# Retention attention and a two-layer MLP on one core: planner lead, buffers, relu engine, tail order and warm-up matmuls changed together

## The chip, the cores and the metric

The kernel runs on one core of one Trainium2 chip. The metric is the device time of one execution in microseconds. Four executions of the kernel before are given; the median is the number to compare with. One of the four was run under the hardware profiler, and all views of the trace come from that one.

Engine names in the profile: PE is TensorE (PEld its weight loads), DVE is VectorE, ACT is ScalarE, POOL is GpSimd, and SP is SyncE, which only issues DMAs here. A name such as SPq means the instruction queue of an engine.

## What is computed

A linear attention with decay per head (a recurrent state), followed by a layer norm without bias, a two-layer MLP with relu, and a residual sum. Shapes: 4 batches, 8 heads, 768 positions, head dimension 64; the model dimension is 512 and the hidden one 2048.

```python
gamma = 1.0 - 2.0 ** (-5.0 - np.arange(H))
for t in range(S):
    state = gamma[None, :, None, None] * state + np.einsum('bhd,bhe->bhde', k[:, :, t], v[:, :, t])
    y[:, :, t] = scale * np.einsum('bhd,bhde->bhe', q[:, :, t], state)
...
x = y.transpose(0, 2, 1, 3).reshape(B, S, H * D)
xn = (x - mean) / np.sqrt(var + 1e-06) * g_ln
out = x + np.maximum(xn @ w_ch1, 0.0) @ w_ch2
```

## The kernel before

**Tiles.** The 768 positions of each batch are six chunks of 128, so there are 24 tiles of 128 positions. Tiles 0 to 3 are the first chunks of the four batches; then come the chunks 1 to 5 of batch 0 (tiles 4 to 8), of batch 1 (9 to 13), batch 2 (14 to 18) and batch 3 (19 to 23). Within a batch the recurrence is done by chunks: scores inside the chunk, and a carried state for what lies before it.

**Attention of one tile.** q, k and v are loaded by GpSimd's DMA queue with a cast from f32 to bf16 (L338), 128 KB each as bf16. For tiles under 10 (`T0`), k and q are transposed on PE (tk, L394; tq, L401) and evacuated by ACT (trk) and DVE (trq, L406). From tile 10 on, k and q share one buffer `qk` and are transposed by a DMA from SP (tr, L416), after which DVE scales q into trq (eq, L423). Then PE makes the scores (pa, L433), DVE multiplies them by the decay mask into asb (am, L440), and PE makes the output (py: the state part on L452, the chunk's own part on L456). For the next chunk's state GpSimd scales v into vg (L509), PE makes k-transposed times vg (pd, L520), and DVE scales it into the state (pb, L534).

**Norm and MLP.** DVE makes the statistics (L490) and the normed xn (L465), ACT keeps a copy of x (L496). xn is transposed on PE (tx, L548) for tiles under 10, by a DMA from SP (ex, L562) after. The first layer (m1, L595) runs in groups of tiles: six groups of one tile, three of two, three of four. Each result is passed through relu into h, by ACT (L608) or DVE (L610). The second layer of each tile is four parts of four matmuls (m2, L632) that sum into one PSUM buffer of the pool `tp`; DVE scales the sum by 1/std, adds x (L640), and SP stores the tile (L647). The last tile's second layer is done in two column halves, and its second half is stored from ACT's queue.

**The order.** The order on each engine is made by a planner when the kernel is built. Each task has an engine (or a choice of two), a cost in ns, a rank, the tasks that it waits for, and the buffer that it takes. The planner repeatedly picks the task that can start first, and among equals the one of lowest rank; the instructions are then written out in that order, and each engine runs its own in that order. Ranks of MLP tasks are 500 plus a unit count, in which one unit stands for one m1 or m2 piece. `rank_of` (L375 to L378) sets the rank of each tile's attention: a number of units (the lead) ahead of the first m1 of its group. Loads are ranked by their order (L356). vg is ranked just ahead of or behind its tile's attention (L512).

**Buffers.** Pools (L166 to L174) give how many buffers of a kind exist: `qk` has 3, `vsb` 5, `vg` 3; in PSUM `tp` and `mm` have 2, `pa`, `py` and `pd` 1. A load waits until the oldest buffer of its pool is free. Besides, each GpSimd load waits for the landing of an earlier one, eight loads before.

**Zero matmuls.** Where the planner sees PE idle before 20 us, `fill` (L99) puts matmuls on zeros there (L656), as many as the gap divided by a time for each: 110 ns for a gap that begins before 6.5 us, 60 ns after. They write a buffer that nobody reads.

Of the kernel before, what the change touches and what calls it, by code (L numbers as in the profile page):

```python
# [14 lines left out]
PE, ACT, DVE, POOL, SP = range(5)  # L15
# [97 lines left out]
def kernel(  # L113
# [19 lines left out]
    DM = H * D  # L133
# [11 lines left out]
    G0 = [sum(GROUPS[:g]) for g in range(NG)]  # L145
    GMAX = max(GROUPS)
    T0 = 10
# [8 lines left out]
    plan = Plan({PE: 330, ACT: 130, DVE: 130, POOL: 130, SP: 0},  # L156
                {PE: 900, ACT: 800, DVE: 900, POOL: 1300, SP: 800}, 2250, 6000)
    ps = bass.MemoryType.PSUM

    def make_pool(name, n, space=None):  # L160
# [6 lines left out]
        name: make_pool(name, n, space)  # L167
        for name, n, space in (
            ("k0", B, None), ("v0", B, None), ("qsb", 6, None), ("ksb", 5, None), ("vsb", 5, None),
            ("qk", 3, None), ("tr", 4, None), ("vg", 3, None), ("trq", 3, None), ("trk", 3, None),  # L170
            ("asb", 2, None),
            ("xn", 4, None), ("xnt", 4, None), ("h1", 2, None), ("osb", 3, None),
            ("tp", 2, ps), ("pa", 1, ps), ("py", 1, ps), ("pd", 1, ps), ("mm", 2, ps),
# [5 lines left out]
    def take(pool, key, shape, dtype):  # L179
        held[pool, key] = pools[pool].tile(shape, dtype, name=pool, tag=pool)  # L180
        return held[pool, key]
# [88 lines left out]
    a = plan.add  # L270
# [32 lines left out]
    def tile_of(kind, t):  # L303
        if kind != "v" and t >= T0:
            return held["qk", t][:, "qk".index(kind)]
        return held[where[kind, t]]
# [55 lines left out]
    unit, u, behind = {}, 0, []  # L362
# [12 lines left out]
    rank_of = {}  # L375
    for t in range(NT):
        g, i = group_of[t]
        rank_of[t] = 10 * t if t < 4 else max(10 * t, 500 + unit["1", g, 0] - (48 if t < T0 else 56) + 8 * i)  # L378


    ex, pbt, vgs, pbs = {}, {}, [], []
# [1 line left out]
    for t in range(NT):  # L383
        b, c = TILES[t]
        r = rank_of[t]
        g, i4 = group_of[t]
# [114 lines left out]
        if c > 0:  # L501
            for cc in ([0, 1] if c == 1 else [c]):
                if cc == C - 1:
                    continue
                j = number[b, cc]

                def e_vg(eng, j=j, cc=cc):
                    e = nc.gpsimd if eng == POOL else nc.vector
                    e.tensor_tensor(  # L509
                        out=take("vg", j, [P, H, D], BF16), in0=tile_of("v", j),  # L510
                        in1=vsc[:, cc, :].unsqueeze(2).to_broadcast([P, H, D]), op=ALU.mult)
                vgt = a(POOL, 1050, r - 2 if cc == 0 else r + 1, e_vg,  # L512
                        [loaded["v", j], vscd] + vgs[-1:], ("vg", j), [where["v", j]])
                vgs.append(vgt)

                def e_pd(eng, j=j, b=b, cc=cc):
                    if cc == 0:
                        take("pd", b, [P, NPAIR, P], FP32)
                    for i in range(NPAIR):
                        nc.tensor.matmul(  # L520
                            held["pd", b][:, i, :], lhsT=tile_of("k", j)[:, 2 * i:2 * i + 2, :],
                            rhs=held["vg", j][:, 2 * i:2 * i + 2, :],
                            start=(cc == 0 and i == 0), stop=(cc == C - 2), skip_group_check=True)
                pdt = a(PE, 230, r - 1 if cc == 0 else r + 2.2, e_pd,
                        [vgt, loaded["k", j]] + ([pbt[j]] if cc else []),
                        ("pd", b) if cc == 0 else None,
                        [("vg", j), where["k", j]] + ([("pd", b)] if cc else []))

                def e_pb(eng, n=number[b, cc + 1], b=b, cc=cc):

                    held["pb", n] = state[len(pbs) % 2]
                    pbs.append(n)
                    for o in (slice(0, D), slice(D, P)):
                        nc.vector.tensor_tensor(  # L534
                            out=held["pb", n][o, :, o], in0=held["pd", b][o, :, o],
                            in1=gch[o, cc, :].unsqueeze(2).to_broadcast([D, NPAIR, D]), op=ALU.mult)
                pbt[number[b, cc + 1]] = a(
                    DVE, 690, r - 1 if cc == 0 else r + 4, e_pb, [pdt, gchd, zerod],
                    ("pb", number[b, cc + 1]), [("pd", b)])
                if cc == 0:  # L540

                    pyt["after"].append(pbt[t])
# [40 lines left out]
    relu, begun = {}, {}  # L583
    for g in range(NG):
        n = GROUPS[g]
        hb, h0 = buf_of[g]
        two = GMAX // n
        for ho in range(0, HO, two):
            key = ("1", g, ho)

            def e_m1(eng, hb=hb, h0=h0, ho=ho, n=n, two=two, key=key):
                p = take("mm", key, [P, two, n * P], FP32)
                for j in range(two):
                    for ko in range(KO):
                        nc.tensor.matmul(p[:, j, :],  # L595
                                         lhsT=w1[:, ko, (ho + j) * P:(ho + j + 1) * P],
                                         rhs=held["xnt", hb][:, h0:h0 + n, ko, :],
                                         start=(ko == 0), stop=(ko == KO - 1))
            m = a(PE, 865, 500 + unit["1", g, ho], e_m1,
                  [ex[t] for t in range(G0[g], G0[g] + n)] + [loaded["w1", ho // 4]],  # L600
                  ("mm", key), [("xnt", hb)])

            def e_re(eng, hb=hb, h0=h0, ho=ho, n=n, two=two, key=key):
                if ho == 0 and h0 == 0:
                    take("h1", hb, [P, HO, GMAX * P], BF16)
                dst, src = held["h1", hb][:, ho:ho + two, h0 * P:(h0 + n) * P], held["mm", key]
                if eng == ACT:
                    nc.scalar.activation(out=dst, in_=src, func=AF.Relu)  # L608
                else:
                    nc.vector.tensor_scalar_max(out=dst, in0=src, scalar1=0.0)  # L610
            first = ho == 0 and h0 == 0
            relu[g, ho] = a({ACT: 600, DVE: 660} if G0[g] < 12 else ACT,
                            600, -10, e_re, [m] + ([] if first else [begun[hb]]),
                            ("h1", hb) if first else None,
                            [("mm", key)] + ([] if first else [("h1", hb)]))
            if first:
                begun[hb] = relu[g, ho]

    for t, cols in [(t, slice(0, DM)) for t in range(NT - 1)] + [
            (NT - 1, slice(i * DM // 2, (i + 1) * DM // 2)) for i in range(2)]:  # L620
        g, i4 = group_of[t]
        hb, h0 = buf_of[g]
        key = ("tp", ("2", t, cols.start))
        w = cols.stop - cols.start
        dep = [relu[g, ho] for ho in range(0, HO, GMAX // GROUPS[g])]
        prev = None
        for part in range(4):
            def e_m2(eng, hb=hb, i=h0 + i4, key=key, part=part, cols=cols, w=w):
                if part == 0:
                    take(*key, [P, w], FP32)  # L630
                for ho in range(4 * part, 4 * part + 4):
                    nc.tensor.matmul(held[key], lhsT=held["h1", hb][:, ho, i * P:(i + 1) * P],  # L632
                                     rhs=w2[:, ho, cols], start=(ho == 0), stop=(ho == HO - 1))
            prev = a(PE, 865 * w // DM, 500 + unit["2", t] + part, e_m2,
                     dep + [loaded["w2", i] for i in range(4) if part == 0] + ([prev] if prev else []),
                     key if part == 0 else None,
                     [("h1", hb)] + ([key] if part else []))

        def e_add(eng, t=t, key=key, cols=cols, w=w):
            nc.vector.scalar_tensor_tensor(  # L640
                out=take("osb", key, [P, w], FP32), in0=held[key], scalar=rstd[:, t:t + 1],
                in1=x_all[:, t, cols], op0=ALU.mult, op1=ALU.add)
        add = a(DVE, 750 * w // DM, -10, e_add, [prev, held["rs", t]], ("osb", key), [key])

        def e_st(eng, t=t, key=key, cols=cols):
            b, c = TILES[t]
            (nc.scalar if eng == ACT else nc.sync).dma_start(out=out_v[b, c, :, cols],  # L647
                                                             in_=held["osb", key])
        a(ACT if cols.start else SP, 350, 100, e_st, [add], uses=[("osb", key)])
# [7 lines left out]
                             start=True, stop=True)  # L657

    with tc.manual_schedule():
        for t in plan.fill(plan.order(), PE, 1100, 20000, lambda at: 110 if at < 6500 else 60, warm):  # L660
            t["emit"](t["eng"])


# [28 lines left out]
```

## Time and profile before

| | us |
|---|---|
| median of four runs | 222.8 |
| the four runs | 228.59, 222.97, 222.34, 222.63 |
| the profiled one among them | 228.59 |
| its span, first to last instruction | 226.8 |
| matmuls on zeros (L656), 121 of them, busy | 11.2 |
| first layer (L595), 768 matmuls, busy | 95.1 |
| second layer (L632), 400 matmuls, busy | 90.4 |
| DVE relu (L610), 9 of them, mean | 0.688 |
| ACT relu (L608), 87 of them, mean | 0.597 |
| DMA transposes of q and k (tr), 14, median to landing | 5.5 |

Times of instructions count from the span's start. The difference between a run's time and its span (here 1.8) lies around the instructions. Busy time of PE is modelled and overlaps from one matmul to the next, so the step from one start to the next is the better measure: 56 ns for 128 columns, 109 for 256, 216 for 512 at full clock. "In turn" below means in an engine's own order. A landing is the time at which the last of a DMA's completions came, which the trace records for each DMA.

### The profile page before, as it was taken

How to read it: one execution, taken by the hardware profiler on the slowest of the kernel's cores; microseconds unless marked ns; L12 is line 12 of the kernel's file. 1: busy time of each engine (PE TensorE's matmuls, PEld its weight loads, DVE VectorE, ACT ScalarE, POOL GpSimd, SP SyncE). 2: the span in 40 equal slices, each digit the busy share in tenths (PEclk: the TensorE clock that was granted, in tenths of full speed). 3: DMA queues.
4: the chain of work that ended last, by engine and by line, in shares of the span. 5: the costliest groups of instructions: out<-in, count | busy, mean ns of one | idle time of the engine just before them, and what ended most of it. 6: DMA issues, size and time to landing. Idle time of an engine off the chain costs nothing.

```text
span 226.8 us, 4691 instructions
## 1 busy us (share of the span) xinstructions
PE 214.6 (95%) x1955; PEld 135.7 (60%) x1955; DVE 117.7 (52%) x229; ACT 86.9 (38%) x170; POOL 89.5 (39%) x105
## 2 busy tenths in 40 slices
PE   6899899999999999989999399999999999999993
PEld 6499899986856566656667135454444444444452
DVE  6435778987669997587895415583111011110121
ACT  5326579874513332223226124356242343333000
POOL 8995699869643784853865000000000000000000
PEclk9679999999999999999999769999999999999999
DMA  8999999999999999999999951201110111101212
GB/s 146 176 179 178 179 158 205 185 154 157 191 83 162 118 141 140 201 196 183 179 124 159 185 102 46 69 19 30 46 45 1 49 46 46 46 12 37 92 46 92
DMA packets 105127, 26.12 MB, mean 115 GB/s; under 512 B 97810, under 2 KB 102162, under 8 KB 105107
## 3 DMA queue, kind: packets, MB, share of 16 engines
q0 software_dynamic: 75984, 13.24, 76.9%
q1 hardware_dynamic: 27938, 12.20, 26.3%
q10 hardware_dynamic: 1184, 0.39, 0.7%
q8 instruction: 15, 0.25, 0.5%
q14 instruction: 6, 0.04, 0.1%
HBM read 27.27 MB, written 6.29 MB: 148 GB/s over the span
## 4 chain that ended last, share of the span: by engine, by line
PE 85%; DMA 9%; DVE 3%; issue 1%; SPq 0%; ACT 0%; DVEq 0%
PE mm L595 35%; PE tp L632 34%; DMA tr<-qk 7%; PE pa L433 3%; PE mm L656 3%; PE py L456 3%; DMA grow<-in_moe_g_ln_dram 2%; PE pd L520 2%; PE py L452 2%; DVE asb L440 2%; PE tp L394 1%; PE tp L401 1%; PE tp L548 1%; PE mm L291 1%; SPq L324 0%
## 5 line engine op out<-in xcount | busy, mean ns | idle before, releaser
L595 PE MATMUL mm<-xnt,w 128*128 128x128 bf16 (+2 forms) x768 | 95.1, 275 | 0.0
L632 PE MATMUL tp<-w,h 128*128 128x512 bf16 (+1 forms) x400 | 90.4, 372 | 0.0
L608 ACT ACTIVATE h<-mm 128x512 bf16<-128x512 f32 x87 | 51.9, 597 | 84.6 <-PE mm L595 84.1
L595 PEld LDWEIGHTS <-w 128*128 128x128 bf16 x768 | 58.9, 98 | 25.1 <-issue 1.7
L632 PEld LDWEIGHTS <-h 128*128 128x128 bf16 x400 | 38.2, 98 | 39.7 <-issue 1.3
L640 DVE SCALAR_TENSOR_TENSOR osb<-tp,rstd,x_all 128x512 f32<-128x512 f32 (+1 forms) x25 | 18.1, 728 | 67.3 <-PE tp L632 67.1
L440 DVE TENSOR_TENSOR asb<-pa,mask 128x1024 bf16<-128x1024 f32 x24 | 29.3, 1220 | 11.6 <-PE pa L433 11.5
L338 POOL DMA_DIRECT2D vsb<-in_v_dram x20 | 18.0, 901 | 12.3 <-PE py L456 9.0
L509 POOL TENSOR_TENSOR vg<-vsb,vsc 128x512 bf16<-128x512 bf16 x16 | 17.0, 1067 | 11.3 <-DMA vsb<-in_v_dram 3.6
L465 DVE SCALAR_TENSOR_TENSOR xn<-py,mv,gb 128x512 bf16<-128x512 f32 x24 | 18.0, 751 | 0.8
L490 DVE BATCH_NORM_STATS2 bns<-py 128x6 f32<-128x512 f32 x20 | 13.9, 695 | 6.6 <-PE py L456 6.5
L496 ACT CAST x_all<-py 128x512 bf16<-128x512 f32 x20 | 11.7, 583 | 14.4 <-DVE xn L465 14.2
L534 DVE TENSOR_TENSOR state<-pd,gch 64x256 bf16<-64x256 f32 x40 | 16.7, 418 | 0.3
L338 POOL DMA_DIRECT2D qk<-in_k_dram x14 | 12.6, 903 | 3.1 <-DMA tr<-qk 2.7
L338 POOL DMA_DIRECT2D qk<-in_q_dram x14 | 12.5, 891 | 1.6 <-DMA w<-in_moe_w_ch_dram 1.6
L656 PE MATMUL mm<-zeros 128*128 128x128 bf16 x121 | 11.2, 264 | 1.0 <-DVE zeros L218 1.0
L456 PE MATMUL py<-vsb,asb 128*128 128x64 bf16 x160 | 8.1, 195 | 3.9 <-DVE asb L440 3.9
L456 PEld LDWEIGHTS <-asb 128*128 128x128 bf16 x192 | 8.2, 101 | 4.0 <-DVE asb L440 4.0
L656 PEld LDWEIGHTS <-zeros 128*128 128x128 bf16 x121 | 9.9, 122 | 1.2 <-DVE zeros L218 1.0
L423 DVE TENSOR_TENSOR trq<-tr,qsc 128x512 bf16<-128x512 bf16 x14 | 6.2, 445 | 7.1 <-DMA tr<-qk 6.9
L610 DVE TENSOR_SCALAR h<-mm 128x512 bf16<-128x512 f32 x9 | 6.2, 688 | 6.5 <-PE mm L595 6.3
L338 POOL DMA_DIRECT2D qsb<-in_q_dram x9 | 8.1, 895 | 1.9 <-PE tp L401 1.6
(68 smaller groups left out, 133.0 us busy)
## 6 DMA issues: line engine op xcount, KB each, us to landing
out_dram<-osb SPq DMA_DIRECT2D x23, 256.0 KB, 2.0
w<-in_moe_w_ch_dram POOLq DMA_DIRECT2D x8, 512.0 KB, 9.5
vsb<-in_v_dram POOLq DMA_DIRECT2D x20, 128.0 KB, 6.4
qk<-in_k_dram POOLq DMA_DIRECT2D x14, 128.0 KB, 5.6
qk<-in_q_dram POOLq DMA_DIRECT2D x14, 128.0 KB, 5.7
qsb<-in_q_dram POOLq DMA_DIRECT2D x9, 128.0 KB, 8.9
ksb<-in_k_dram POOLq DMA_DIRECT2D x6, 128.0 KB, 9.1
k<-in_k_dram POOLq DMA_DIRECT2D x3, 128.0 KB, 7.4
```

Of the source, the lines that this page charges most:

```text
L338: nc.gpsimd.dma_start(out=tile_of(kind, j), in_=src)
L440: nc.vector.tensor_tensor(out=take("asb", t, [P, NPAIR, 2, P], BF16).rearrange("p i a t -> p a i t"), in0=held["pa", t], in1=mask.rearrang ...
L456: nc.tensor.matmul(py[:, h, :], lhsT=held["asb", t][:, h // 2, h % 2, :], rhs=tile_of("v", t)[:, h, :], start=(mi == 0), stop=(mi == n - 1))
L465: nc.vector.scalar_tensor_tensor(out=take("xn", t, [P, DM], BF16), in0=held["py", t].rearrange("p h d -> p (h d)"), scalar=mv[:, t, 0:1], ...
L490: nc.vector.bn_stats(out=bns[:, t, :], in_=held["py", t].rearrange("p h d -> p (h d)"))
L509: e.tensor_tensor(out=take("vg", j, [P, H, D], BF16), in0=tile_of("v", j), in1=vsc[:, cc, :].unsqueeze(2).to_broadcast([P, H, D]), op=ALU. ...
L534: nc.vector.tensor_tensor(out=held["pb", n][o, :, o], in0=held["pd", b][o, :, o], in1=gch[o, cc, :].unsqueeze(2).to_broadcast([D, NPAIR, D ...
L595: nc.tensor.matmul(p[:, j, :], lhsT=w1[:, ko, (ho + j) * P:(ho + j + 1) * P], rhs=held["xnt", hb][:, h0:h0 + n, ko, :], start=(ko == 0), s ...
L608: nc.scalar.activation(out=dst, in_=src, func=AF.Relu)
L632: nc.tensor.matmul(held[key], lhsT=held["h1", hb][:, ho, i * P:(i + 1) * P], rhs=w2[:, ho, cols], start=(ho == 0), stop=(ho == HO - 1))
L640: nc.vector.scalar_tensor_tensor(out=take("osb", key, [P, w], FP32), in0=held[key], scalar=rstd[:, t:t + 1], in1=x_all[:, t, cols], op0=AL ...
L656: nc.tensor.matmul(held["mm", "warm"][:, 0:P], lhsT=zeros, rhs=zeros, start=True, stop=True)
```

## The change

Six edits are made together.

1. The pool `qk` gets four buffers instead of three.
2. The lead of the attention ahead of its group's first m1 is 48 units for all tiles; before it was 48 for tiles under 10 and 56 from tile 10 on.
3. The vg of tile 4 gets a rank ahead of all remaining loads on GpSimd.
4. DVE may take a relu only for groups that begin before tile 6; before, for groups that begin before tile 12.
5. In the ranks of the last tile's second layer, the parts of the second half come after all of the first half's; before, the two halves took turns.
6. The number of zero matmuls is computed with 110 ns for gaps that begin before 11.5 us and 80 after.

```diff
-            ("qk", 3, None), ("tr", 4, None), ("vg", 3, None), ("trq", 3, None), ("trk", 3, None),
+            ("qk", 4, None), ("tr", 4, None), ("vg", 3, None), ("trq", 3, None), ("trk", 3, None),
...
-        rank_of[t] = 10 * t if t < 4 else max(10 * t, 500 + unit["1", g, 0] - (48 if t < T0 else 56) + 8 * i)
+        rank_of[t] = 10 * t if t < 4 else max(10 * t, 500 + unit["1", g, 0] - 48 + 8 * i)
...
-                vgt = a(POOL, 1050, r - 2 if cc == 0 else r + 1, e_vg,
+                vgt = a(POOL, 1050, -500 if j == 4 else r - 2 if cc == 0 else r + 1, e_vg,
                         [loaded["v", j], vscd] + vgs[-1:], ("vg", j), [where["v", j]])
...
-            relu[g, ho] = a({ACT: 600, DVE: 660} if G0[g] < 12 else ACT,
+            relu[g, ho] = a({ACT: 600, DVE: 660} if G0[g] < 6 else ACT,
                             600, -10, e_re, [m] + ([] if first else [begun[hb]]),
...
-            prev = a(PE, 865 * w // DM, 500 + unit["2", t] + part, e_m2,
+            prev = a(PE, 865 * w // DM, 500 + unit["2", t] + part + (4 if cols.start else 0), e_m2,
                      dep + [loaded["w2", i] for i in range(4) if part == 0] + ([prev] if prev else []),
...
-        for t in plan.fill(plan.order(), PE, 1100, 20000, lambda at: 110 if at < 6500 else 60, warm):
+        for t in plan.fill(plan.order(), PE, 1100, 20000, lambda at: 110 if at < 11500 else 80, warm):
             t["emit"](t["eng"])
```

Because the planner reads ranks, buffers and costs, the edits move tasks on every engine, not only those that they name. In the built order the zero matmuls go from 121 to 86. On GpSimd the vg of tile 4 stands between v of tile 6 and k of tile 7, and k of tile 13 is issued between the vg of tiles 9 and 10. On PE the pd of tile 9 follows directly on the pa of tile 8, where before it followed on the py of tile 8. On DVE the trq of later tiles still stands ahead of the asb of earlier ones in many places, for example those of tiles 14 and 15 ahead of the asb of tile 13. On SP the tr of tiles 21 and 22 follow each other.

## What I predict, before the result

> **What bounds the kernel now.** I read four views in this order: the page, the chain of waits in order of time, the timelines of PE and POOL, and the busy time in stretches. First the page:
>
> ```profile
> span 226.8 us, 4691 instructions
> PE 214.6 (95%) x1955; PEld 135.7 (60%) x1955; DVE 117.7 (52%) x229; ACT 86.9 (38%) x170; POOL 89.5 (39%) x105
> PEclk9679999999999999999999769999999999999999
> ```
>
> PE is the bound: 95% of the span, so a gain has to come out of PE's own work or out of its few gaps. The clock row shows half speed at the start and once more at the 23rd and 24th of the 40 slices. The chain says where PE isn't doing useful work (start, duration, what):
>
> ```profile
> 10.69 2.03 PE mm L656 x19
> ...
> 13.89 2.43 PE mm L656 x36
> ...
> 88.45 8.46 DMA tr<-qk
> ...
> 120.74 6.51 DMA tr<-qk
> 127.27 0.42 DVE trq L423
> 127.72 1.24 DVE asb L440
> 129.00 0.61 PE py L456 x8
> 129.61 3.41 PE mm L595 x8
> 133.03 4.00 PE tp L632 x16
> ```
>
> L656 are matmuls on zeros, which only pass time. The two `tr<-qk` pieces are DMA transposes that the chain followed back to; how much PE lost there is in its timeline, in brackets behind the instruction that waited:
>
> ```profile
> 98.66 0.40 PE L433 MATMUL pa<-trq,tr 64*128 64x128 bf16 x8 [0.95 <-DVE asb L440]
> 129.00 0.61 PE L456 MATMUL py<-vsb,asb 128*128 128x64 bf16 x8 [3.87 <-DVE asb L440]
> ```
>
> So stall 1 (tile 16) costs about 1.1 us from issue to issue, stall 2 (tile 20) 4.0. The name DVE asb hides the cause: in VectorE's order the trq of a later tile (L423, 127.27) stands ahead of the asb of tile 20 (L440, 127.72), and it waits for the transpose of tile 21. After stall 2 eight 512-column matmuls take 3.41 instead of the 1.73 of the chain's other pieces, and the next sixteen 4.00 instead of 3.45: another 2.2. The stretches confirm it (after the busy times: clock, DMA share, GB/s):
>
> ```profile
> 95.00:100.00 5.00, 4.05 (x47) 2.42 (x46) 3.04 (x4) 0.00 (x0) 1.79 (x2) 1.00 1.87 204
> 125.00:130.00 5.00, 1.13 (x13) 0.71 (x11) 2.00 (x3) 0.55 (x1) 0.00 (x0) 0.72 1.71 187
> 130.00:135.00 5.00, 5.00 (x16) 1.83 (x14) 1.28 (x3) 1.67 (x3) 0.00 (x0) 0.60 0.53 107
> ```
>
> **The profiled run isn't the typical one.** It took 228.59 (226.8 of span and 1.8 around it), the other three runs 222.34 to 222.97. Taking stall 2 and its slow clock out, 4.0 + 2.2 = 6.2, leaves 222.4: the other runs fit a kernel with stall 1 and without stall 2. I count from 222.4; the median shown, 222.8, lies 0.4 above.
>
> **What the Trainium skill says.** "TensorE: Matmul & The Clock Gate", Part 1: the clock is full or half, decided over free-running windows of 3413 ns. The trace agrees: its clock record has one half-clock stretch of 6.83 us (two windows) from 127.2, and zeros cost 107 ns each before 14.5 us and 56 after. The page asks for a whole idle window; here 2.0 us idle (125.1 to 127.2) were enough, and the trace decides. "Perfetto Trace Analysis", Per-engine timelines: VectorE and ScalarE are strict FIFO; the trq that held up asb agrees. "DMA: Bandwidth & Descriptors", Issuing engines are not separate DMA queues: loads from GpSimd and transposes from SyncE share 16 engines. It agrees: loads landed 0.6 to 0.9 us apart before 57 us, but 1.8 apart from 91.0 to 96.6 (v17 to q17), with transposes in flight.
>
> **Part by part.**
>
> *Fewer zeros.* 121 become 86. Those that go: 9 before the first py, 1 and 17 before tile 2's transposes, then 2, 2, 1 and 3. The first py could go when asb of tile 0 was ready at 11.0 (9.76 + 1.23); nineteen zeros kept it until 12.71, ten end at 11.76: 0.95 gained. Nineteen in place of 36 then run to 14.7 instead of 16.3, the data of tile 2 having landed at 12.3; behind them the k and xnt evacuations on ScalarE (0.58 each) just keep up. Tile 0's first L595 comes at about 16.25 instead of 17.90, the second at 18.6 instead of 20.40. So PE is 1.8 ahead at 20 us. The weights don't hold it: the third quarter of w1 landed at 22.4 and is used from 23.3.
>
> *Where that goes.* GpSimd is paced by landings until 56 us: each load waits for the landing of the eighth before it, and loads land back to back.
>
> ```profile
> 46.16 0.87 POOL L338 DMA_DIRECT2D qk<-in_q_dram  x1 [1.63 <-DMA w<-in_moe_w_ch_dram]
> ...
> 53.43 0.90 POOL L338 DMA_DIRECT2D vsb<-in_v_dram  x1
> 54.32 2.08 POOL L509 TENSOR_TENSOR vg<-vsb,vsc 128x512 bf16<-128x512 bf16 x2
> ```
>
> The first of the two vg is tile 9's, ready at 55.4 whatever PE does. Its pd was at 56.14 to 56.5 on PE, behind py of tile 8. In the new order it directly follows pa of tile 8:
>
> ```profile
> 53.60 0.40 PE L433 MATMUL pa<-trq,trk 64*128 64x128 bf16 x8
> ...
> 55.90 0.40 PE L456 MATMUL py<-vsb,asb 128*128 128x64 bf16 x8
> 56.14 0.39 PE L520 MATMUL pd<-vg,ksb 128*128 128x128 bf16 x4
> ```
>
> By order alone that pa comes 1.5 later than before (more work ahead of it), minus 1.8: at 53.3, done at 53.7. PE then stands until 55.4, 1.7 us, and does pd, tx, tk and py to 56.5; before, the same amount of work was done at 56.7. So of 1.8 about 0.2 is left. VectorE wouldn't let py go much earlier: the first add (0.75) now stands between m2 of tile 0 and asb of tile 8 (1.23), 2.2 after the pa began.
>
> *Lead of 48, and qk from 3 to 4.* With equal PE work I counted where each pa falls. Tiles 9 to 13 come 4.5 to 0.9 us earlier, 15 to 17 1.5 to 2.6 later, 18 and 19 5.2, 20 8.4, 21 6.9, 22 3.5, 23 10.4 later. Loads come earlier, because k of tile 13 needs no free buffer: 55.4 instead of 62.5. Following GpSimd's new order with its own durations (0.9 a load, 1.05 a vg), q22 is issued near 112 instead of 119.8; with 6 to landing and 5.5 for the transpose (the medians) tile 22's is there by 124, needed after 130. So stall 2 goes with room to spare. Tile 16's q is issued near 77, lands at 82.5, its transpose at 88 (5.5) to 91 (8.5, as in stall 1); its trq stands ahead of asb of tile 14 and must start by 88.6. So in place of stall 1, 1.1, I take 0.4, with 0 and 2.5 as ends.
>
> *vg of tile 4 ahead of tile 7's loads.* It delays k7 by 1.07; with eight loads outstanding the DMA queue hides it, and k7 lands 34.2 for a use at 36. Cost 0; without the cover, 1.
>
> *relu on ScalarE from tile 6.* One relu (0.69) leaves VectorE at 61.6, where ScalarE is over half idle. 0.
>
> *Last halves in order.* Half 0 of the last tile finishes four parts (1.7) earlier and its store leaves the end. Half 1 still ends PE's order, and its add (0.48) wasn't held up by that of half 0. 0.1, bounds 0 and 0.4.
>
> Sum on the profiled run: 228.59 - 6.2 (stall 2) - 0.2 (start) - 0.7 (stall 1 less its rest) - 0.1 (end) = 221.4. Against the typical 222.4 it is 1.0 less, 0.4%; against the median shown 0.6%.
>
> **The rivals.**
>
> *The new gap drops the clock (slower).* Place: the 1.7 us between pa and pd of tile 8 at 53 to 55. A gap of 1.1 (stall 1) left the clock at 1.00, one of 2.0 by the window's end halved it for 6.83 us. If 1.7 is enough, matmuls run at half speed to 62: 3.4 lost, which nothing gives back, since PE has no slack after. 221.4 + 3.4 = 224.8. It decides once the idle share of one window passes a limit between 1.1/3.41 = 32% and 2.0/3.41 = 59%; 1.7 is 50%, if it falls in one window. For it: it is past the middle. Against: a window boundary can split it.
>
> *The head start is kept (faster still).* GpSimd gets to vg of tile 9 early, or PE arrives late and finds it: 1.6 more, 219.8. Against: landing times pace GpSimd there.
>
> *The lead doesn't do what it says (no change).* Loads bunch earlier (k15 to q17 between 66 and 80), transposes take their 8.5 instead of 5.5, and tiles 15, 16 and 18 stall about as much as stall 1 did plus some: 222.7.
>
> **How the numbers follow.** Forecast 55%, range of its own 220.5 to 222.4; clock drop 20%; head start kept 10%; no change 15%. This kernel's measurement can tell 0.3%, 0.7 us: faster means below 222.1, slower above 223.5. Faster: 0.48 of the forecast, all of the head start: 0.58. Same: 0.07 and 0.13, 0.20. Slower: the clock drop and the tail of the third rival, 0.22. The range takes in head start and clock drop: 219.7 to 225.0.
>
> **What would show it.** L656 x86; first L595 near 16.3; a bracket of about 1.7 on PE's L520 near 55; no wait over 1 us on tr after 100 us; the clock at 1.00 from 15 us to the end. Wrong, if PE passes tile 9's pd without a gap, if the clock row shows a dip near slice 10, or if a tr wait of over 2 us stands between 80 and 110.

## The result, and the profile after

The changed kernel takes 224.05 us (median of 43 executions, 222.39 to 225.99), the kernel before 223.09 (64 executions beside them). The ratio is 1.0056, with a 95% interval of 1.004 to 1.0073: slower by about 1.2 us (1.0 by the medians), where 1.0 less was forecast. The medians are of all executions, the ratios, here and below, only of those not over 1.5% above the fastest of the same kernel, so the two can differ by half a per cent. The profiled execution took 223.81.

From the page: span, busy time and instructions of each engine, granted clock in 40 slices, and two groups (busy, mean ns of one, idle time before them and what ended it).

```profile
span 222.0 us, 4620 instructions
...
PE 210.5 (95%) x1920; PEld 132.7 (60%) x1920; DVE 117.5 (53%) x229; ACT 87.5 (39%) x170; POOL 89.5 (40%) x105
...
PEclk9999999999799999999999999999999999999999
...
L338 POOL DMA_DIRECT2D qk<-in_k_dram x14 | 12.9, 920 | 5.9 <-DMA tr<-qk 5.8
...
L656 PE MATMUL mm<-zeros 128*128 128x128 bf16 x86 | 8.3, 262 | 1.0 <-DVE zeros L218 1.0
```

PE is still the bound at 95%. The 86 zeros are there, and the dip of the 23rd and 24th slice, with its wait of 4.0 at tile 20, is gone. A new dip stands in the 11th slice. And GpSimd's loads of k waited 5.8 us for a DMA transpose, a row to come back to.

The timeline of PE, with the idle time in brackets, at the two places that cost time:

```profile
52.03 0.40 PE L433 MATMUL pa<-trq,trk 64*128 64x128 bf16 x8
54.90 0.58 PE L520 MATMUL pd<-vg,ksb 128*128 128x128 bf16 x4 [2.47 <-DMA vsb<-in_v_dram]
...
84.82 0.38 PE L452 MATMUL py<-state,trq 128*128 128x128 bf16 x4
85.67 0.41 PE L456 MATMUL py<-vsb,asb 128*128 128x64 bf16 x8 [0.47 <-DVE asb L440]
...
94.00 0.41 PE L456 MATMUL py<-vsb,asb 128*128 128x64 bf16 x8 [0.76 <-DVE asb L440]
```

Place one is the gap in front of the pd of tile 9, with half clock behind it, as the busy times by stretch show (PE first; the number after the engines is the clock):

```profile
50.00:54.60 4.60, 2.43 (x18) 1.10 (x17) 3.90 (x8) 0.88 (x2) 4.32 (x5) 1.00 2.48 156
54.70:58.10 3.40, 3.20 (x32) 3.00 (x32) 0.83 (x2) 1.07 (x2) 3.23 (x5) 0.50 2.08 136
58.20:62.00 3.80, 3.80 (x41) 2.92 (x39) 2.69 (x5) 2.16 (x4) 3.01 (x4) 1.00 1.71 210
```

The bracket of the pd names a load of v, but v of tile 9 had landed at 51.2; what ended last is the vg of tile 9, which ran on GpSimd from 53.77 to 54.85.

Place two are the waits of tiles 13 and 14. Counted from start to start against the steps of undisturbed matmuls, they cost 0.9 (0.26 of it ahead of the L452 at 84.82) and 0.9. VectorE's timeline tells what held the asb:

```profile
81.47 0.42 DVE L423 TENSOR_TENSOR trq<-tr,qsc 128x512 bf16<-128x512 bf16 x1 [2.87 <-DMA tr<-qk]
...
84.07 0.41 DVE L423 TENSOR_TENSOR trq<-tr,qsc 128x512 bf16<-128x512 bf16 x1
84.40 1.22 DVE L440 TENSOR_TENSOR asb<-pa,mask 128x1024 bf16<-128x1024 f32 x1
...
92.27 0.43 DVE L423 TENSOR_TENSOR trq<-tr,qsc 128x512 bf16<-128x512 bf16 x1 [3.11 <-DMA tr<-qk]
92.72 1.23 DVE L440 TENSOR_TENSOR asb<-pa,mask 128x1024 bf16<-128x1024 f32 x1
```

The trq at 81.47, 84.07 and 92.27 are those of tiles 14, 15 and 16, the asb those of tiles 13 and 14. VectorE stood 2.87 and 3.11 us in front of a later tile's trq. Behind the first wait its own work had piled up (statistics, add and norm, 2.1 us, not shown), then came the trq of tile 15, so that the asb of tile 13 began at 84.40, though its scores were there at 82.03. Behind the second stood the asb of tile 14. The transposes of tiles 14, 15 and 16 landed at 81.4, 82.6 and 92.2. Why they were late is in GpSimd's timeline:

```profile
53.77 1.08 POOL L509 TENSOR_TENSOR vg<-vsb,vsc 128x512 bf16<-128x512 bf16 x1
...
63.93 0.94 POOL L338 DMA_DIRECT2D vsb<-in_v_dram  x1 [1.33 <-PE py L456]
69.78 0.87 POOL L338 DMA_DIRECT2D qk<-in_k_dram  x1 [4.91 <-DMA tr<-qk]
70.64 0.88 POOL L338 DMA_DIRECT2D qk<-in_q_dram  x1
```

The load at 69.78 is k of tile 14. With four buffers I had taken it to overwrite tile 10's, whose transpose had landed at 60.0. It waited 4.91 us, until just after the transpose of tile 13 had landed (69.2): the build gave it tile 13's buffer, the one freed last.

In the kernel before, with three buffers, it was no better: k of tile 14 was given tile 13's buffer there too, whose transpose landed at 72.9, and went out at 73.74. But there VectorE's order put the asb of tile 13 ahead of the trq of tile 14, and PE lost nothing at these tiles. From the GpSimd and VectorE timelines of before:

```profile
73.74 0.94 POOL L338 DMA_DIRECT2D qk<-in_k_dram  x1
```

```profile
82.56 1.22 DVE L440 TENSOR_TENSOR asb<-pa,mask 128x1024 bf16<-128x1024 f32 x1
...
87.17 0.41 DVE L423 TENSOR_TENSOR trq<-tr,qsc 128x512 bf16<-128x512 bf16 x1
```

So the change didn't make that load late; it left it late, and put operations that wait for it ahead of ones that are due.

### The profile page after: what moved, and what is told of

The parts are those of the page before. It is cut to its first block, busy times and chain, and to the rows that moved or that the text cites. A ratio compares the mean times of both kernels' runs of the same rounds, so it can differ in the third digit from the quotient of the medians.

```text
span 222.0 us, 4620 instructions
## 1 busy us (share of the span) xinstructions
PE 210.5 (95%) x1920; PEld 132.7 (60%) x1920; DVE 117.5 (53%) x229; ACT 87.5 (39%) x170; POOL 89.5 (40%) x105
## 4 chain that ended last, share of the span: by engine, by line
PE 68%; DMA 22%; POOL 4%; DVE 3%; issue 2%; POOLq 0%
PE tp L632 32%; PE mm L595 28%; DMA w<-in_moe_w_ch_dram 8%; DMA tr<-qk 5%; DMA vsb<-in_v_dram 5%; DMA ksb<-in_k_dram 4%; PE pa L433 2%; PE py L456 2%; PE pd L520 2%; PE py L452 1%; DVE asb L440 1%; POOL vg L509 1%; POOL qsb L338 1%; POOL qk L338 1%; DVE osb L640 1%
## 5 line engine op out<-in xcount | busy, mean ns | idle before, releaser
L595 PE MATMUL mm<-xnt,w 128*128 128x128 bf16 (+2 forms) x768 | 94.1, 273 | 1.1 <-DMA w<-in_moe_w_ch_dram 1.1
L632 PE MATMUL tp<-w,h 128*128 128x512 bf16 (+1 forms) x400 | 89.0, 371 | 0.0
L608 ACT ACTIVATE h<-mm 128x512 bf16<-128x512 f32 x87 | 52.0, 598 | 83.3 <-PE mm L595 83.2
L595 PEld LDWEIGHTS <-w 128*128 128x128 bf16 x768 | 58.5, 98 | 25.4 <-DMA w<-in_moe_w_ch_dram 1.5
L338 POOL DMA_DIRECT2D vsb<-in_v_dram x20 | 17.8, 896 | 5.8 <-PE py L456 4.5
L338 POOL DMA_DIRECT2D qk<-in_k_dram x14 | 12.9, 920 | 5.9 <-DMA tr<-qk 5.8
L338 POOL DMA_DIRECT2D qk<-in_q_dram x14 | 12.6, 901 | 1.5 <-DMA w<-in_moe_w_ch_dram 1.5
L656 PE MATMUL mm<-zeros 128*128 128x128 bf16 x86 | 8.3, 262 | 1.0 <-DVE zeros L218 1.0
L338 POOL DMA_DIRECT2D qsb<-in_q_dram x9 | 8.1, 899 | 1.1 <-PE pd L520 0.6
L184 ACT COPY xnt<-tp 128x512 bf16<-128x512 bf16 x10 | 5.8, 585 | 5.7 <-PE tp L548 5.6
```

What stands on the lines that cost most here:

```text
L338: nc.gpsimd.dma_start(out=tile_of(kind, j), in_=src)
L595: nc.tensor.matmul(p[:, j, :], lhsT=w1[:, ko, (ho + j) * P:(ho + j + 1) * P], rhs=held["xnt", hb][:, h0:h0 + n, ko, :], start=(ko == 0), s ...
```

## The experiments

Two theories after reading the traces: the gap and its half clock at 55 us are the loss, or the late transposes are. Medians in us; the ratio is to the kernel before in runs alongside, with its 95% interval. The kernel before had medians of 222.55 to 223.06 there, so a difference of medians between two rows, or from the change (224.05), is good to about half a microsecond. Where it matters, the difference of the ratios is given too, in us of 223.

| run | what | median | ratio |
|---|---|---|---|
| e1 | change, pd of tile 9 behind py of tile 8 | 225.75 | 1.0146 (1.0097 to 1.0195) |
| e2 | change, qk buffers in turn | 221.91 | 0.9929 (0.9891 to 0.9966) |
| e3 | change, asb ahead of later trq | 221.63 | 0.9953 (0.9931 to 0.9976) |
| e4 | change, all three | 219.25 | 0.9837 (0.9796 to 0.9878) |
| e5 | change without edit 3 (vg) | 221.79 | 0.9979 (0.9939 to 1.0018) |
| e6 | change without edit 1 (qk 4) | 222.03 | 0.9993 (0.9961 to 1.0024) |
| e7 | change without edit 2 (lead) | 230.45 | 1.0404 (1.0349 to 1.0458) |
| e8 | change without edit 6 (zeros) | 224.38 | 1.0129 (1.008 to 1.0178) |
| e9 | before, a second trace | 224.23 | one execution |
| e10 | before, asb ahead of later trq | 222.11 | 1.0001 (0.9973 to 1.0029) |
| e11 | before with edit 2 alone | 220.89 | 0.9924 (0.9898 to 0.995) |
| e12 | before with edit 1 alone | 223.41 | 0.9994 (0.9959 to 1.0029) |
| e13 | change, buffers and asb | 221.93 | 0.9958 (0.9931 to 0.9985) |
| e14 | change, buffers and pd | 221.22 | 0.9917 (0.9885 to 0.9949) |
| e15 | before with edit 3 alone | 223.39 | 1.0021 (0.9993 to 1.0048) |

**e1: close the gap.** In the planner only, the pd of tile 9 is told to come after the py of tile 8. (The planner then also moves a few pieces of the layers and relus on PE and ScalarE; GpSimd's order stays.)

```diff
+        last_py = pyt if t else None
         pyt = a(PE, 240 + (220 if c else 0), r + 3.2, e_py,
...
-                        [vgt, loaded["k", j]] + ([pbt[j]] if cc else []),
+                        [vgt, loaded["k", j]] + ([pbt[j]] if cc else []) + ([last_py] if j == 9 else []),
```

> The changed kernel (224.05) with one thing altered: the pd of tile 9 is placed behind the py of tile 8 again. Gap theory: the 2.6 us gap on PE at 52.3 to 54.9 and the half-clock window behind it (about 1.5) are the loss; the clock stays at 1.00 and the time falls by 1.5 (clock alone) to 4.1 (gap too), so 220.0 to 222.5. Late-transpose theory: what is won at 55 us is waited for again at the asb of tiles 13 and 14, whose two waits grow from 0.9 each to 2 or more; the time is 223.4 to 224.1.

It came out slower than the change, at 225.75, above the ranges of both theories: that the gap alone is the loss falls. PE passes the pd of tile 9 without a gap and at full clock, and begins the next L596 at 54.91, where the change began that L595 at 57.42; GpSimd then waits longer for the same landing, and PE stands at tile 13. GpSimd's and PE's timelines of this run:

```profile
61.36 0.94 POOL L338 DMA_DIRECT2D vsb<-in_v_dram  x1
69.54 0.87 POOL L338 DMA_DIRECT2D qk<-in_k_dram  x1 [7.24 <-DMA tr<-qk]
```

```profile
79.11 1.90 PE L633 MATMUL tp<-w,h 128*128 128x512 bf16 x8
83.93 0.38 PE L452 MATMUL py<-state,trq 128*128 128x128 bf16 x4 [2.91 <-ACT x_all L497]
84.78 0.41 PE L456 MATMUL py<-vsb,asb 128*128 128x64 bf16 x8 [0.47 <-DMA qk<-in_k_dram]
```

The k of tile 14 goes out at 69.54 as against 69.78, the py of tile 13 at 84.78 as against 85.67: of the 2.5 won before, 0.9 is left. That wait then brought its own half clock, 3.41 us from 85.85, and a wait of 0.80 at tile 18 came on top, so the run ended later than the change.

**e2: the four qk buffers in turn.**

```diff
+    qkr = [ctx.enter_context(tc.tile_pool(name=f"qk_{i}", bufs=1)) for i in range(plan.bufs["qk"])]
+
     def take(pool, key, shape, dtype):
-        held[pool, key] = pools[pool].tile(shape, dtype, name=pool, tag=pool)
+        src = qkr[(key - T0) % len(qkr)] if pool == "qk" else pools[pool]
+        held[pool, key] = src.tile(shape, dtype, name=pool, tag=pool)
```

> The changed kernel with the four qk buffers used in turn, so that k of tile 14 overwrites tile 10's buffer and not tile 13's. k of tile 14 is issued near 65 instead of 69.8, q of tile 15 near 69 instead of 73.4, and the transpose of tile 15 lands near 78 instead of 82.6. Late-transpose theory: the wait on asb of tile 13 (1.0) goes, the one of tile 14 stays or goes; 222.1 to 223.2. Gap theory: the gap and the clock dip at 55 us are unchanged, and no more than the 1.0 is won; if the transposes were not what the asb waited for, 224.

The order of instructions is unchanged on every engine; 2.1 us are won (2.8 by the ratios), more than either theory gave it. GpSimd's timeline (three lines were added to the code, so L341 is the L338 of before):

```profile
65.00 0.88 POOL L341 DMA_DIRECT2D qk<-in_k_dram  x1
```

k of tile 14 goes out at 65.00, with no wait in brackets. The transposes of tiles 15 and 16 land at 80.1 and 87.7 instead of 82.6 and 92.2, and PE has no wait left behind tile 9. The gap and the half clock at 55 us are all there still.

**e3: asb ahead of later trq.**

```diff
-            eq = a(DVE, 490, r, e_eq, [ek, qscd, eq], ("trq", t), [("tr", t)])
+            eq = a(DVE, 490, r, e_eq, [ek, qscd, eq, am], ("trq", t), [("tr", t)])
```

> The changed kernel with the trq of each tile from 10 on placed behind the asb of the tile before it on VectorE, so that an asb never stands behind a trq that waits for a later tile's transpose. Late-transpose theory: both waits at tiles 13 and 14 (1.9 together) go, 222.1, and the loss against the kernel before is more than made up. If the same transposes are then waited for by the pa of tiles 15 and 16 themselves, 223.5 to 224.1. Gap theory: the gap and dip at 55 us stay, so it stays above 222.

221.63, 2.4 won (2.3 by the ratios). VectorE now begins the asb of tile 13 at 82.04, ahead of the trq of tile 14, and that of tile 14 at 90.08; the planner moves some other work with it. The transposes are as late as in the change (tile 15 at 83.2, tile 16 at 91.0), and no wait over 0.6 us stands on PE between tile 9 and the end. So here the late landing costs nothing by itself; it costs because the order on VectorE puts a trq that waits for it ahead of an asb that is due.

**e4: all three.**

> The three edits of the other runs together: pd of tile 9 behind py of tile 8, qk buffers in turn, asb ahead of later trq. If the gap with its clock window (1.5 to 4.1) and the two waits (1.9) are separate losses, 218.1 to 220.7, faster than the kernel before by 1 to 2 per cent. If loads take back what is won, 222 to 223.

219.25, 4.8 less than the change and 1.6% less than the kernel before: the fastest here. PE's timeline at the place of the gap:

```profile
52.26 0.40 PE L436 MATMUL pa<-trq,trk 64*128 64x128 bf16 x8
...
54.30 0.41 PE L459 MATMUL py<-vsb,asb 128*128 128x64 bf16 x8 [0.53 <-DMA qk<-in_q_dram]
54.55 0.39 PE L404 MATMUL tp<-idn,qsb 128*128 128x128 bf16 x4
54.77 0.39 PE L524 MATMUL pd<-vg,ksb 128*128 128x128 bf16 x4
```

Instead of 2.47 us of idle time a wait of 0.53 is left, and behind it PE's timeline shows no bracket to the end. The same edit that made e1 slower is worth 2.7 here (221.93 of e13 less 219.25, and 2.7 by the ratios), once nothing later takes it back. The pair of pd and asb without the buffers was not run, so what the buffers add to these two is not known.

**e5 to e8: the change less one edit each,** by the lines of the diff above.

> The change without its edit 3 (vg of tile 4 ahead): pd of tile 9 stands behind py of tile 8, and on VectorE only the trq of tile 14, not 15, can stand near asb of tile 13; trq of 16 and 17 stand ahead of asb of 15. Fixed-transposes theory (k of tile 14 waits for the transpose of tile 13 and so fixes when tiles 15 and 16 can go on, whatever PE did before): no gap at 55, but what it gives is waited for at tiles 13 to 15; 223 to 226. Gap theory: 1.5 to 4 less than the changed kernel, 220.0 to 222.5.

> The change without its edit 1 (three qk buffers as before). Fixed-transposes theory: k of tile 13 is issued after 62 instead of 54.8, so its transpose and with it k of tile 14 come some 3 to 5 later; the wait in front of asb of tile 14 (behind trq of tile 15) grows to 3 or more, and the time is 225 to 228. If the fourth buffer brings nothing because tile 14 takes the buffer of tile 13 anyway: 223.7 to 224.4. Gap theory: as the changed kernel, 224.

> The change without its edit 2 (lead 56 from tile 10 on). On VectorE trq of 15 stands behind asb of 13, and ahead of asb of 14. Fixed-transposes theory: the wait at tile 13 goes, those at tiles 14 and 15 become 0 to 2, since the attention of these tiles is now asked for 3 to 5 units earlier; 222 to 225. If lead 48 is what removed the wait of tile 20, a wait of about 4 after 100 us comes back: 226 to 228. Gap theory: 224, with the gap at 55 as it was.

> The change without its edit 6: the order of everything else is that of the changed kernel, with 121 zero matmuls. PE comes 1.8 later to the pd of tile 9, so the gap there shrinks to about 0.8 and the clock stays full. Fixed-transposes theory: PE has made up for the late start by tile 13, and the waits at tiles 13 and 14 end at the same times as in the changed kernel (their sum grows or shrinks by what the clock dip took); 223.0 to 224.4. If the earlier start is worth its 1.8 at the end: 225.8.

*Without vg (e5)* 221.79, 2.3 won (1.7 by the ratios). That lies in the gap theory's range, and the gap at 55 us is gone; but the orders on all engines change with edit 3, and two of them touch the other theory, so this run can't tell the two apart: k of tile 14 stands one place earlier on GpSimd and is given tile 10's buffer, so that it goes out at 61.6 instead of 69.8; and no trq of a later tile stands ahead of the asb of tile 13. What is left is a wait of 1.58 at the pd of tile 4 and one of 2.01 at tile 18.

*Without the fourth buffer (e6)* 222.03, 2.0 won (1.4 by the ratios), where 1 to 4 more or nothing was expected. With three buffers GpSimd's timeline reads

```profile
63.27 0.88 POOL L338 DMA_DIRECT2D qk<-in_k_dram  x1
67.30 0.94 POOL L338 DMA_DIRECT2D qk<-in_k_dram  x1
```

These are k of tiles 13 and 14. The first is 8.5 later than with four, the second 2.5 earlier: it took a buffer whose transpose (tile 11's) had landed at 62.3. So with four buffers this load goes out later than with three. But that is not what PE gains by: the transpose of tile 14 landed at 81.1 (81.4 with four), that of tile 15 at 88.7 (82.6). The orders changed too, and VectorE's timeline shows the likelier reason why PE is spared, though no run separates the two:

```profile
80.50 1.22 DVE L440 TENSOR_TENSOR asb<-pa,mask 128x1024 bf16<-128x1024 f32 x1 [0.67 <-PE pa L433]
81.64 0.41 DVE L423 TENSOR_TENSOR trq<-tr,qsc 128x512 bf16<-128x512 bf16 x1
...
88.72 0.43 DVE L423 TENSOR_TENSOR trq<-tr,qsc 128x512 bf16<-128x512 bf16 x1 [2.25 <-DMA tr<-qk]
89.17 1.22 DVE L440 TENSOR_TENSOR asb<-pa,mask 128x1024 bf16<-128x1024 f32 x1
```

The asb of tile 13 stands ahead of the trq of 14 and 15, and that of tile 14 behind the trq of 15, no longer of 16.

*Without the lead (e7)* 230.45, 6.4 more, above the 226 to 228 expected. VectorE stands 5.37 us for the transpose of a later tile, and PE at tile 18 behind it; first VectorE's timeline, then PE's:

```profile
115.40 0.43 DVE L423 TENSOR_TENSOR trq<-tr,qsc 128x512 bf16<-128x512 bf16 x1 [5.37 <-DMA tr<-qk]
```

```profile
117.02 0.61 PE L456 MATMUL py<-vsb,asb 128*128 128x64 bf16 x8 [3.64 <-DVE asb L440]
```

The clock is half for 6.83 us from 116.14. That is the kind of wait of stall 2, at another tile, and with edit 2 it is gone.

*Without the zeros edit (e8)* 224.38. PE's timeline:

```profile
52.19 0.40 PE L433 MATMUL pa<-trq,trk 64*128 64x128 bf16 x8
54.50 0.38 PE L520 MATMUL pd<-vg,ksb 128*128 128x128 bf16 x4 [1.92 <-DMA vsb<-in_v_dram]
...
84.14 0.38 PE L452 MATMUL py<-state,trq 128*128 128x128 bf16 x4 [1.16 <-ACT x_all L496]
84.99 0.41 PE L456 MATMUL py<-vsb,asb 128*128 128x64 bf16 x8 [0.47 <-DVE asb L440]
...
94.25 0.41 PE L456 MATMUL py<-vsb,asb 128*128 128x64 bf16 x8 [1.69 <-DVE asb L440]
```

With 121 zeros PE is at the pa of tile 8 at 52.19 as against 52.03, the gap did not shrink to 0.8, and the clock stayed full here. Yet the py of tiles 13 and 14 come at 84.99 and 94.25 as against 85.67 and 94.00: the 1.5 that no half clock took are waited away in front of them. By the medians edit 6 is worth 0.3, by the two ratios 0.7%; its size stays open between these (0.3 and 1.6 us).

**e9 to e12 and e15: the kernel before, and one edit on it.**

> The kernel before, unchanged, for a second trace of it. If the wait of 4.0 at tile 20 was of that one execution, this one shows stall 1 (about 1.1 at tile 16), little at tile 20, and a time of 222 to 223; if the wait belongs to every execution, it stands here too and the time is above 226. The start: half clock until about 14 and py of tile 2 near 21 if that belongs to the 121 zeros, near 18 if the clock was full early.

> The kernel before with the trq of each late tile placed behind the asb of the tile before. If the trq in VectorE's order is what turns a late transpose into a wait of PE, stall 1 (1.1) goes: 221.2 to 222.0. If the late tiles' own scores then wait as long, 222.5 to 223.2.

> The kernel before with edit 2 alone (lead 48 for the late tiles). If the shorter lead is by itself what takes the waits on transposes away, 221.2 to 222.2; if it pays only together with the other edits, 222.5 to 224.

> The kernel before with edit 1 alone (four qk buffers). Here the built order gives k of tile 14 tile 10's buffer, so k of 13 goes out near 55 and k of 14 near 62, 10 earlier than before. If early loads are what matters, stall 1 goes: 221.2 to 222.0. If the other lead (56) or a later tile then waits, 222.5 to 225.

> The kernel before with edit 3 alone. The gap at pd of tile 4 (0.8 to 1.6 at 29 us in the traces of the kernel before) goes, one of 2 or more at pd of tile 9 comes; the offset behind tile 9 is then 0.4 (without a clock dip) to 2 (with one) worse than before. If late transposes of tiles 15 to 17 decide there too, 222 to 223.5 whatever the gap does; if the gap decides, 223.2 to 225.

*e9:* no 4.0 at tile 20 this time, but a larger stall 1 (1.75) and four small waits (0.37, 0.37, 0.42, 0.61) between 94 and 127 us. From its PE timeline, stall 1:

```profile
99.47 0.40 PE L433 MATMUL pa<-trq,tr 64*128 64x128 bf16 x8 [1.75 <-DVE asb L440]
```

*e11:* the lead alone gives 220.89, a little better than its range, and one wait of 1.03 is left on PE behind 50 us. Of the three edits tried alone on the kernel before it is the only one that helps. *e10* shows no gain by the ratio, though its median is 0.95 lower: late landings still cost there, since the pa of tiles 16 and 17 themselves wait (0.52 and 1.03). *e12* sends k of tile 14 out at 63.3 instead of 72.9, and then waits 2.12 at tile 19; no gain shows. *e15* moves the gap: none at the pd of tile 4, 1.85 at that of tile 9, and 1.69 at tile 19; no difference that the interval shows.

**e13 and e14: two of the three fixes.**

> The three fixes (219.25) without the one of pd: qk buffers in turn and asb ahead of later trq, pd of tile 9 directly behind pa of tile 8. If gap and clock window count once the transposes are on time: 2 to 3 more than 219.25, so 221.3 to 222.2. If they are made up for later, 219.3 to 220.

> The three fixes without the one of trq: buffers in turn and pd of tile 9 behind py of tile 8. With the buffers in turn the transpose of tile 15 lands near 79.6, just where asb of tile 13 wants to start. If late transposes are all there is: a wait of 0 to 1.5 in all, 219.2 to 221. If the order of trq and asb costs by itself, above 221.5.

*e13* keeps the gap and has no wait of note behind it: 221.93, so once transposes are on time the gap with its half clock counts, 2.7. Its 22 times fall in two groups, nine from 220.21 to 220.73 and thirteen from 221.85 to 222.65, with nothing between; e2, with the same gap, has five up to 220.86 and seven from 221.87. The profiled one of e13 (222.32) has a half-clock window of 3.41 us from 54.35. The step of about 1.6 fits one such window. e6 supports this: it has the same gap, its times fall in two such groups, and its profiled one (220.48), of the lower group, has no half clock at the gap. The rest up to e4, 1.1, would then be the gap itself; that is a sum, not a run. *e14* is left with one wait of 0.56 at tile 14, 0.7 from start to start: 221.22, 2.0 above e4 and between its two ranges, and its 12 times spread from 219.96 to 221.93. Only its lowest are explained by that wait; why the others are slower stays open.

## Why the prediction was wrong

*The step that failed* is that of the lead and the fourth buffer: "Following GpSimd's new order with its own durations". I followed the order, but took the buffer of each load from the planner's model, oldest first, as "Buffers" above has it. The first half of the step held: "k of tile 13 needs no free buffer: 55.4" (54.8). Then k of tile 14 was given the buffer freed last and went out at 69.8, and tile 16's q was issued at 81.0, not near 77; its transpose landed at 92.2, not 88 to 91. In place of the 0.4 that I took stand 0.9 and 0.9 at tiles 13 and 14, 1.4 more than taken, though within the bounds of 0 to 2.5. With the 0.7 of the baseline, below, that is 2.1 of the 2.7 by which the sum of 221.4 fell short; the remaining half a microsecond was not traced. e2 changes the buffers and nothing else, and wins 2.1, which turns slower into faster. I had seen that trq of 14 and 15 stand ahead of asb of 13, and priced it only for tile 14; e3 shows that this order is the other half of the cause.

*vg of tile 4 ahead*, cost 0, was wrong in the same way. Its k7 was not the point; as built, the edit decides which buffer tile 14 gets, and where pd of tile 9 stands. Without it, 2.3 less (e5), though which of these counts e5 can't say.

*The baseline* of 222.4 was 0.7 too low: stall 2 was indeed not in each execution, but others lose time on transposes in other places (e9), and the kernel before has a median of 223.09.

*The zeros.* The first L595 came at 13.7, not 16.25, and the start of the trace is 3 us ahead of that of before; but e8 with 121 zeros is nearly as early (py of tile 2 at 18.12, after 17.98, before 21.13). What differed was the clock: full from 6.9 and 5.4 in these two, half from 7.7 to 14.5 in the trace of before, a stretch that the prediction's "one half-clock stretch" passed over, so it took 107 ns a zero for a property of the kernel. "The weights don't hold it" failed too: with the clock full early, the second L595 piece waits for weights, and so takes back what fewer zeros gave (change, then e8, from PE's timelines):

```profile
17.08 1.07 PE L595 MATMUL mm<-xnt,w 128*128 128x128 bf16 x16 [0.94 <-DMA w<-in_moe_w_ch_dram]
```

```profile
17.22 1.07 PE L595 MATMUL mm<-xnt,w 128*128 128x128 bf16 x16 [0.37 <-DMA w<-in_moe_w_ch_dram]
```

With half clock until about 14 and 86 zeros (e1, e2) that py comes at 18.77 and 19.03. So the edit saves about 2 in an execution that starts cold for as long, as forecast, and 0.1 in one that doesn't. That the gain is handed back at tile 9 held: e2 is 1.05 behind the change at the py of tile 2, and both begin the pd of tile 9 at 54.9.

*The gap* of 1.7 was 2.6 from start to start, since PE came at 52.0 and not at 53.3; the vg was ready at 54.85, close to the 55.4 taken. *The rival of the clock drop* saw the place and the mechanism, with 3.41 us of half clock and 1.5 lost instead of 6.83 and 3.4; but in the change it decided nothing, since e1 and e8, without it at 55 us, are no faster. That its 224.8 lies near the measured 224.05 is chance. *"The lead doesn't do what it says"* named the bunched loads and stalls at 15, 16 and 18; they came at 13 and 14. But the lead does what it says: 6.4 in e7, and by itself about 0.8% in e11. That stall 2 goes was right. The edits for relu and for the last halves weren't tried alone.

## What to carry to other kernels

A planner's model of a buffer pool is not the pool: before pricing one buffer more, look up in the built kernel which transfer the load really waits for; here the load that mattered got the buffer freed last. On an in-order engine put the operation that is due ahead of the one that waits for a later tile's transfer; a late landing then cost nothing in e3, though in e10 the late tiles themselves still waited. And a wait that is fixed by transfers swallows what is won ahead of it, so remove the last one first: the same move of pd cost time in e1 and gave 2.7 between e13 and e4.

## What the runs showed of the hardware

*The clock drops on less than a whole idle window, and by chance of phase.* The Trainium skill, "TensorE: Matmul & The Clock Gate", Part 1, says that the windows are free-running and that the warm-up therefore varies from run to run. The same held for the drop here: a gap of about 2.5 us at the same place was followed by one window of half clock in the trace of after and not in that of e6. In the trace of after the clock changes at 54.68, and the window back from there, 51.27 to 54.68, holds all but the last 0.2 us of the gap. In e6 a change at 6.25 puts a window's end at 54.04, within its gap from 52.16 to 54.68, and the clock stayed full. These two windows (PE's busy time is the first after the length):

```profile
51.27:54.68 3.41, 1.16 (x12) 0.52 (x11) 2.66 (x5) 0.21 (x1) 3.41 (x4) 1.00 2.53 155
```

```profile
50.63:54.04 3.41, 1.53 (x14) 0.68 (x13) 3.03 (x6) 0.58 (x1) 3.41 (x5) 1.00 2.46 155
```

That page puts the drop after at least one idle window; here 2.25 us without work in a window of 3.41 were enough, and the measurement decides.

*The limit lies between 1.46 and 1.53 us of busy time in a window.* Cut each of the 17 traces into windows of 3.413 us, counted from one of its own clock changes. From 14 us on, every window with PE busy for 1.46 us or less (e13, just below the limit) was followed by half clock, and none at full clock with 1.53 or more (e6, just above) was. So an idle share of about 56% of one window is the estimate from these traces; busy times are modelled, so it is good to a few hundredths of a microsecond at best. The prediction had it between 32% and 59%.
